# Token inputs transposed two blocks ahead of their splits, and raw token weights loaded later

## The chip, the cores and the metric

The kernel runs on one core of a Trainium2 chip. The metric is the device time of one execution in microseconds (us). Five engines work side by side, each through its own list of instructions in order: TensorE (PE in the rows; PEld is its weight load), VectorE (DVE), ScalarE (ACT), GpSimd (POOL) and SyncE (SP), which here issues every DMA. An instruction may wait on a semaphore of another engine or of a DMA, and then everything behind it on its own engine waits too.

## What is computed

Three layers follow each other on 4 batches of 576 tokens, 512 wide:

```python
scores = scale * np.matmul(q, k.transpose(0, 1, 3, 2))          # 8 heads of 64
bias = np.maximum(x @ w1 + b1, 0.0) @ w2                        # 576 x 576 per head, from positions
attn = softmax(scores + bias);  x = np.matmul(attn, v)          # to 4 x 576 x 512

xt = x.transpose(0, 2, 1)                                       # token mixing
h = np.maximum(xt @ w_tok1, 0.0) @ w_tok2                       # 576 -> 256 -> 576
u = x + h.transpose(0, 2, 1)
x = u + np.maximum(u @ w_ch1, 0.0) @ w_ch2                      # channels, 512 -> 1536 -> 512

# then a gated layer: w_in, tanh form, normalisation, w_sg over tokens, w_out, residual
```

The weights of the second layer reach the kernel as 64-bit floats, seen as pairs of 32-bit words.

## The kernel before, in words

**Attention.** The work is cut into 80 units: a batch, a pair of heads and a block of 128 query tokens (the fifth block has 64). The first 20 units (U0) are batch 0, during which the bias is also made. A unit goes through `scores` (L444: TensorE products `ss`, then a DVE pass at L465 that adds the bias and finds the extreme), `softmax` (L474, ACT), `divisor` and `divided` (L483 to L495, POOL and DVE), `turn_z` and `turn` (L511, L530: TensorE transposes into `z`, `x`, `y`, copied out to `zA`, `xA`, `yA` by ACT or DVE), and `values` (L547: TensorE products `o`, moved to X by `place`, L437). Units -3 to 15 run one at a time in `single` (L704), units 16 (PA) to 77 two at a time in `double` (L752), and units 78 and 79 by the lines after the loops (L808 on). The order of the work is the order of these lines; no planner moves it.

**Bias.** 36 groups of 16 rows are made on TensorE (`bps`), copied by ACT into a staging tile `bst` (L379) and sent by DMA into `bias_m` (L385). Each `single` up to n = 11 makes two. The DVE pass of `scores` waits for the rows of its block.

**Loads.** `loads(n)` (L680) issues all other transfers of unit n on the SP list, behind that unit's bias transfers: K and Q blocks (`kr`, `qr`, four DMAs each, L264), V, and at n = WL (9) the first two raw tiles of the token weights (L95).

**Token weights.** `Jobs` (L64) turns a raw 64-bit tile (`wraw`, two buffers) into a high and a low part. There are seven token jobs: two and a short one for w_tok1, four for w_tok2. A job is worked off in four pieces (`piece`, L158): the ACT square L132 with the DVE operation L133, then L139, L144, L149; the ACT copy L105 and the DVE subtraction L113 of the finished job come with the pieces of the next. A piece is called in `single` for n = 14 and 15 (L742) and at the end of 20 of the 31 `double` calls (L797). What is left is done after the first half of the token product (L831).

**Token inputs.** For batch 0 the tokens are five blocks (0 to 3 and NM, the short one). `x_part` (L616) makes four TensorE transposes of a block into a PSUM tile `px` and then splits it into a high part (ACT, L61) and a low part (DVE, L62), both into space of `bias_m` that is no longer read. A `px` tile holds two blocks and comes from `s_tile` (L353), which deals out two PSUM buffers in turn; `ss`, `px` and the product tiles `ph` share them. `early_x` (L639) takes one or two blocks:

```python
def early_x(ts):
    px = s_tile("px")
    for i, t in enumerate(ts):
        x_part(0, t, x0, px[:, i])
```

It is called with block 0 before the values of units 76 and 77 (L810), and with blocks 1 and 2, then 3 and NM, after the transposes of units 78 and 79 (L824). Then come the values of 78 and 79, the two halves of the first token product (`tok1`, L625, 14 matmuls each into `ph`), the rest of the weight jobs, and `tok1_out` (L633, ACT and DVE), on which the second token product (`pu`, L908) waits.

Of the kernel before, what the change touches and what calls it, by code (L numbers as in the profile page):

```python
# [19 lines left out]
def kernel(ctx, tc, ins, consts, out, dbg=None, nb=4, stop=None):  # L20
# [4 lines left out]
    B, H, N, HD = q.shape  # L25
    P = 128
    NP = H // 2
    NM = N // P
# [30 lines left out]
    def split(src, hi, lo, eng=None):  # L59

        S.copy(out=hi, in_=src)  # L61
        (eng or V).tensor_tensor(out=lo, in0=src, in1=hi.bitcast(F32), op=ALU.subtract)  # L62

    class Jobs:  # L64
# [8 lines left out]
        def add(self, key, nm, rows, cols, fold, dst, times=1):  # L73

            t = ins[nm][rows, cols]
            if fold > 1:
                t = t.rearrange("(a p) c w -> p a c w" if wide[nm] else "(a p) c -> p a c", a=fold)
            else:  # L80
                t = t.rearrange("p (a c) w -> p a c w" if wide[nm] else "p (a c) -> p a c", a=1)
            self.queue.append((key, t, wide[nm], dst, times))
# [110 lines left out]
    U, U0 = len(units), NP * NS  # L193
# [51 lines left out]
    for i in range(NP // 2):  # L245
        t = pp.tile([P, 2 * N + TL], F32, tag="p", name="kraw0")
# [108 lines left out]
    def s_tile(name):  # L355
        flip[0] ^= 1
        return ps_s.tile([P, 2, 512], F32, tag=f"s{1 - flip[0]}", name=name)

    t = pp.tile([P, 2 * N + TL], F32, tag="p", name="early")
# [84 lines left out]
    def scores(n, between):  # L444
        b, p, it = units[n]
        qt, kt = queries.pop(n), keys[b, p]
        na = 2 if it < NM else 1
        if na == 2:
            flip[0] = 0
        ss = [s_tile("ss") for a in range(na)]  # L450

        for hf in range(2):
            js = slice(hf * HN, (hf + 1) * HN)
            for m in range(na):
                for a in range(2):
                    r, o = halves[a], halves[m if na == 2 else a]
                    T.matmul(  # L457
                        ss[a % na][o, hf, 0:HN], lhsT=qt[r, m * HD:(m + 1) * HD], rhs=kt[r, js], start=True, stop=True
                    )
        bias = [bias_m[:, it, 2 * p + a] for a in range(2)] if na == 2 else [bias_t[:, p]]  # L460
        pr = pp.tile([P, 2 * N + TL], F32, tag="p", name="pr")
        mn = sm_p.tile([P, 2], F32, tag="mn", name="mn")
        sm = sm_p.tile([P, 2], F32, tag="sm", name="sm")
        for a in range(na):
            V.tensor_tensor_reduce(  # L465
                out=pr[:, a * NB:a * NB + N].rearrange("p (f n) -> p f n", f=2), in0=ss[a][:, :, 0:HN],
                in1=bias[a].rearrange("p (f n) -> p f n", f=2),
                scale=scale, scalar=BIG, op0=ALU.add, op1=ALU.min, accum_out=mn[:, a:a + 1],
            )
            if a == 0:  # L470
                between()
        return pr, mn, sm, na
# [24 lines left out]
    def normalise(*s):  # L497
        divisor(*s)
        divided(*s)
# [17 lines left out]
    def z_out(n, z, r):  # L517
        zs = rooms[0][2][:, n % 2]
        S.copy(out=zs[r], in_=z[r])
        if units[n][2] < NM:  # L520
            for i in range(2):
                G.tensor_copy(out=zwA[halves[i], n % 2], in_=zs[halves[1 - i], HD:P])
# [20 lines left out]
    def y_out(ys, y):  # L543
        if y is not None:
            V.tensor_copy(out=ys, in_=y)  # L545
# [32 lines left out]
    def hide(gi):  # L578
        if gi < GALL:
            hs[gi] = hidden(groups[gi])  # L580
# [32 lines left out]
    bias_place(groups[GUP - 1], bps)  # L613
    gnext = GUP

    def x_part(b, t, xs, px):  # L616

        w = min(P, N - t * P)
        c0 = b * N + t * P
        for d in range(ND):  # L620
            T.transpose(px[0:w, d * P:(d + 1) * P], X[:, d, c0:c0 + w], ident)

        split(px[0:w], xs[0][0:w, t], xs[1][:, t] if w == P else xs[0][w:2 * w, t])

    def tok1(xs, m, ph):  # L625
        ms = slice(m * P, (m + 1) * P)
        for t in range(NM):
            for n, (i, j) in enumerate(TERMS):
                T.matmul(ph, lhsT=t1[i][:, t, ms], rhs=xs[j][:, t], start=t == 0 and n == 0, stop=False)  # L629
        T.matmul(ph, lhsT=t1[0][:, NM, ms], rhs=xs[0][:, NM], start=False, stop=False)  # L630
        T.matmul(ph, lhsT=t1[1][:, NM, ms], rhs=xs[0][:, NM], start=False, stop=True)
# [7 lines left out]
    def early_x(ts):  # L639
        px = s_tile("px")  # L640
        for i, t in enumerate(ts):
            x_part(0, t, x0, px[:, i])

    tokw = t1 = t2 = None
    wjobs = Jobs(stg, 2)
# [14 lines left out]
            )  # L660
    KL, QL, KT, QT = 11, 10, 7, 6
    st = {}
    PA, PB, WL = U0 - 4, U - 2, 9

    def k_blocks(n):
        for m in range(NP, len(pairs)):
# [37 lines left out]
    def single(n):  # L704
        nonlocal gnext
        gs = []
        if n >= -3 and gnext < GALL:
            gs = list(range(gnext, min(gnext + 2, GALL)))
            gnext += 2
        st[n + 3] = scores(n + 3, (lambda: normalise(*st[n + 2])) if n + 2 >= 0 else (lambda: None))  # L710
        if len(gs) > 0:
            hide(gs[0] + 2)
        if n >= 0:
            z = ps_t.tile([P, 1, P], F32, tag="z", name="z")
            z_out(n, z[:, 0], turn_z(n, st[n][0], z[:, 0]))
            x_out, ys, y = turn(n, st[n][0])
            x_out()
        qs = s_tile("bps") if 0 <= n + 5 < U0 else None
        zq = None if qs is None else qs[:, 0, HN:HN + P]
        q_turn(n + 5, zq)  # L720
        bp = [bias_product(gi, hs.pop(gi), qs if gi == gs[0] else None) for gi in gs]
        if qs is not None and not gs:
            q_out(n + 5, zq)
        softmax(*st[n + 3], which=(0,))
        if n >= 0:
            y_out(ys, y)
        for gi, ps in zip(gs, bp):
            bias_place(groups[gi], ps)
            if gi == gs[0]:
                q_out(n + 5, zq)  # L730

        late = n > 0
        if late and not gs:
            add = values(n - 1)
        softmax(*st[n + 3], which=(1,))
        if late and gs:
            add = values(n - 1)
        if len(gs) > 1:
            hide(gs[1] + 2)
        k_blocks(n)  # L740
        q_blocks(n)
        if n > PA - 3:  # L742
            wjobs.piece()
        if late:
            add()
        st.pop(n - 1, None)
        loads(n)

    def two_values(n):
        return [values(n, "xz"), values(n + 1, "oy")]  # L750
# [56 lines left out]

    flat = bias_m.rearrange("p i h n -> p (i h n)").bitcast(F32R)  # L808
    x0 = [flat[:, i * NS * DM:(i + 1) * NS * DM].rearrange("p (t n) -> p t n", t=NS) for i in range(2)]
    early_x([0])  # L810
    adds = two_values(PB - 2)
    normalise(*st[U - 1])
    for add in adds:
        add()
    z = ps_t.tile([P, 1, P], F32, tag="z", name="z")
    z_out(PB, z[:, 0], turn_z(PB, st[PB][0], z[:, 0]))
    x_out, ys, y = turn(PB, st[PB][0])
# [3 lines left out]
    z_out(U - 1, z[:, 0], turn_z(U - 1, st[U - 1][0], z[:, 0]))  # L821
    x_out, _, _ = turn(U - 1, st[U - 1][0], "o")
    x_out()
    early_x([1, 2])  # L824
    early_x([3, NM])
    for add in two_values(PB):
        add()
    wjobs.need(("t1", NM // 2))
# [67 lines left out]
    if True:  # L896
# [22 lines left out]
        for b in range(nb):  # L919
# [17 lines left out]
            xs = new_x() if b + 1 < nb else None  # L937
# [471 lines left out]
```

## Time and profile before

| what | us |
|---|---|
| median of 3 runs | 885.73 (885.43 to 885.96) |
| the profiled execution, whole | 884.51 |
| its span, first to last instruction | 882.6 |
| PE busy | 867.3 (98% of the span) |
| DVE, ACT, POOL busy | 623.3, 420.8, 231.7 |
| mean granted TensorE clock | 0.997 of full |

All times in rows are microseconds from the start of the span. A row of the timeline reads: start, duration, engine, source line, operation, output<-input, partitions x elements, how many of them were merged, and in brackets how long the engine stood idle just before and what ended that. PE's matmuls are pipelined: the duration of one reaches into the next. The granted clock is a share of full speed (2.4 GHz).

### The profile page before, as it was taken

Reading aid. Unit: us, or ns where it says so; the run is one execution under the profiler, and the core shown is the slowest. Engines: PE = TensorE matmul, PEld = TensorE weight load, DVE = VectorE, ACT = ScalarE, POOL = GpSimd, SP = SyncE. Lnnn points to the kernel's source line nnn. Section 1 sums busy time; section 2 is a strip of 40 time slices with the busy share of each in tenths; the row PEclk is TensorE's granted clock in tenths of the full one; section 3 lists DMA queues with packets and bytes.
Section 4 is the critical chain, followed back from the end, with each engine's and each line's share of the span. In section 5 each row is a group of like instructions: output and inputs, shape, how many; then the busy total and the mean of one; then the engine's idle time right before and its main releaser. Section 6 shows DMA issues by size and latency. Waiting matters only on the chain.

```text
span 882.6 us, 22049 instructions
## 1 busy us (share of the span) xinstructions
PE 867.3 (98%) x8962; PEld 767.3 (87%) x8962; DVE 623.3 (71%) x1429; ACT 420.8 (48%) x955; POOL 231.7 (26%) x440
## 2 busy tenths in 40 slices
PE   8999999999999899999999999999999999999998
PEld 4466688788888789999999999999998989889996
DVE  7899788888787579989836453522218989887756
ACT  7999778888888634343313122212115522322310
POOL 1345467666766400000000000000002422322230
PEclk9999999999999999999999999999999999999999
DMA  8965643344332032234301100000041001010002
GB/s 189 192 138 130 138 80 60 69 76 85 59 65 53 3 96 69 76 117 127 107 34 49 48 25 25 25 1 1 1 81 48 25 1 48 1 61 1 1 13 95
DMA packets 120149, 55.38 MB, mean 63 GB/s; under 512 B 101872, under 2 KB 108656, under 8 KB 120048
## 3 DMA queue, kind: packets, MB, share of 16 engines
q1 hardware_dynamic: 119888, 53.85, 25.5%
q8 instruction: 70, 1.15, 0.6%
q14 instruction: 31, 0.25, 0.1%
q10 hardware_dynamic: 160, 0.13, 0.1%
HBM read 38.62 MB, written 4.72 MB: 49 GB/s over the span
## 4 chain that ended last, share of the span: by engine, by line
PE 86%; DVE 8%; ACT 3%; issue 1%; DMA 1%; POOL 0%; ACTq 0%; DVEq 0%; POOLq 0%
PE a L1040 17%; PE pg L876 17%; PE ss L457 9%; PE o L559 5%; PE pu L1207 5%; PE ps L1229 5%; PE po L1260 4%; PE pv L1154 4%; PE x L535 4%; PE y L540 3%; PE bps L366 3%; PE o L560 2%; PE z L514 2%; PE pu L908 1%; PE ph L629 1%
## 5 line engine op out<-in xcount | busy, mean ns | idle before, releaser
L1040 PE MATMUL a<-g,c 128*128 128x384 f32 x864 | 161.5, 334 | 0.0
L1040 PEld LDWEIGHTS a<-g,c 128*128 128x128 f32 x864 | 151.1, 188 | 0.0
L492 POOL TENSOR_SCALAR pr<-pr,sm 128x576 f32<-128x576 f32 (+2 forms) x208 | 131.2, 648 | 49.6 <-DVE sm L485 42.1
L883 DVE SCALAR_TENSOR_TENSOR g<-pg,g 128x384 fp32r<-128x384 f32 x72 | 40.1, 556 | 146.7 <-ACT g L882 146.7
L876 PE MATMUL pg<-u,c 128*128 128x384 f32 x720 | 134.5, 334 | 0.0
L876 PEld LDWEIGHTS pg<-u,c 128*128 128x128 f32 x720 | 125.7, 188 | 0.1
L882 ACT ACTIVATE g<-pg 128x384 fp32r<-128x384 f32 x72 | 35.3, 491 | 182.6 <-PE pg L876 175.1
L478 ACT ACTIVATE pr<-pr,mn 128x576 f32<-128x576 f32 x144 | 112.4, 780 | 8.0 <-DVE mn L465 6.4
L465 DVE CUSTOM_DVE_ANT_0 pr<-ss,bias_m 128x576 f32<-128x576 f32 x128 | 94.2, 750 | 21.5 <-PE ss L457 17.0
L62 POOL TENSOR_TENSOR y<-X,y 128x576 fp32r<-128x576 f32 x4 | 6.1, 1555 | 367.1 <-ACT y L61 367.1
L559 PE MATMUL o<-xA,vm 64*64 64x128 f32 (+1 forms) x1280 | 80.4, 264 | 0.0
L559 PEld LDWEIGHTS o<-xA,vm 64*64 64x64 f32 x1280 | 69.8, 135 | 10.9 <-issue 5.5
L457 PE MATMUL ss<-kt,X 64*64 64x288 f32 x864 | 71.8, 410 | 0.0
L995 DVE STREAM_TRANSPOSE res<-X 32x256 f32<-32x256 f32 (+1 forms) x176 | 68.2, 387 | 2.9
L560 PE MATMUL o<-yA,vm 64*64 64x128 f32 x1024 | 69.9, 275 | 0.0
L132 ACT ACTIVATE sq<-wraw 128x512 f32<-128x512 f32 (+2 forms) x43 | 27.9, 648 | 66.4 <-DVE w L149 54.7
L560 PEld LDWEIGHTS o<-yA,vm 64*64 64x64 f32 x1024 | 57.7, 134 | 0.7 <-DVE yA L545 0.2
L1229 PE MATMUL ps<-wsT,vn 128*128 128x288 f32 x384 | 56.4, 295 | 0.0
L347 DVE TENSOR_SCALAR X<-ttab,wsm 128x576 f32<-128x576 f32 x108 | 55.3, 572 | 0.1
L1229 PEld LDWEIGHTS ps<-wsT,vn 128*128 128x128 f32 x384 | 52.8, 188 | 0.3 <-POOL vn L62 0.3
L1207 PE MATMUL pu<-y,wi 128*128 128x288 f32 x384 | 51.8, 295 | 1.0 <-ACT uT L1211 1.0
L1207 PEld LDWEIGHTS pu<-y,wi 128*128 128x128 f32 x384 | 51.3, 188 | 1.6 <-ACT uT L1211 1.3
(168 smaller groups left out, 1652.1 us busy)
## 6 DMA issues: line engine op xcount, KB each, us to landing
wraw<-in_moe_w_ch_dram SPq DMA_DIRECT2D x24, 512.0 KB, 3.6
bias_m<-bst SPq DMA_DIRECT2D x32, 288.0 KB, 4.0
vm<-in_v_dram SPq DMA_DIRECT2D x32, 128.0 KB, 2.7
wraw<-in_moe_w_in_dram SPq DMA_DIRECT2D x8, 512.0 KB, 3.6
out_dram<-res SPq DMA_DIRECT2D x16, 256.0 KB, 2.0
kr<-in_k_dram SPq DMA_DIRECT2D x48, 72.0 KB, 2.4
qr<-in_q_dram SPq DMA_DIRECT2D x48, 72.0 KB, 2.5
wraw<-in_moe_w_out_dram SPq DMA_DIRECT2D x4, 512.0 KB, 3.4
```

Of the source, the lines that this page charges most:

```text
L347: V.tensor_scalar(out=hd, in0=tt, scalar1=b1i, scalar2=None, op0=ALU.min)
L457: T.matmul(ss[a % na][o, hf, 0:HN], lhsT=qt[r, m * HD:(m + 1) * HD], rhs=kt[r, js], start=True, stop=True)
L465: V.tensor_tensor_reduce(out=pr[:, a * NB:a * NB + N].rearrange("p (f n) -> p f n", f=2), in0=ss[a][:, :, 0:HN], in1=bias[a].rearrange("p ...
L478: S.activation(out=pr[:, a * NB:a * NB + N], in_=pr[:, a * NB:a * NB + N], func=AF.Exp, scale=-1.0, bias=mn[:, a:a + 1], accum_out=sm[:, a ...
L492: G.tensor_scalar(out=pr[:, dc:dc + hi - lo], in0=pr[:, lo:hi], scalar1=sm[:, a:a + 1], scalar2=1.0, op0=ALU.mult, op1=ALU.mult,)
L559: T.matmul(o[0:HD, 0:w], lhsT=vm[r, t, 0], rhs=xs[r, t, 0:w], start=st_, stop=en)
L560: T.matmul(o[HD:P, 0:w], lhsT=vm[r, t, 1], rhs=rh[r], start=st_, stop=en)
L876: T.matmul(pg, lhsT=c1[f][i][:, d], rhs=u[j][:, d], start=d == 0 and n == 0, stop=d == ND - 1 and n == 2)
L995: V.transpose(out=o, in_=src(c)[32 * a:32 * a + 32])
L1040: T.matmul(acc[d], lhsT=c2[f][i][:, d * P:(d + 1) * P], rhs=g[j], start=f == f0 and n == 0, stop=f == f1 and n == 2,)
L1207: T.matmul(pu[:, hf, 0:HN], lhsT=wi[i][:, d, f * P:(f + 1) * P], rhs=y[j][:, d, js], start=d == 0 and m == 0, stop=d == ND - 1 and m == 2,)
L1229: T.matmul(ps[:, hf, 0:HN], lhsT=vn[i][:, t, ds_], rhs=wsT[j][:, t, js], start=t == 0 and m == 0, stop=False,)
```

## The change

Five things are edited. `x_part` is cut into `x_turn` (transposes) and `x_split`; `early_x` transposes all its blocks first and returns the splits to be called later. Block 1 is now transposed with block 0, before the values of units 76 and 77, and split after them; blocks 2 and 3 share a tile, and NM has one for itself. `WL` becomes U0 - 6 = 14. The two calls of `piece` in `single` are gone.

```diff
+    def x_turn(b, t, px):
+        c0 = b * N + t * P
         w = min(P, N - t * P)
-        c0 = b * N + t * P
         for d in range(ND):
             T.transpose(px[0:w, d * P:(d + 1) * P], X[:, d, c0:c0 + w], ident)
 
+    def x_split(t, xs, px):
+        w = min(P, N - t * P)
         split(px[0:w], xs[0][0:w, t], xs[1][:, t] if w == P else xs[0][w:2 * w, t])
...
     def early_x(ts):
         px = s_tile("px")
         for i, t in enumerate(ts):
-            x_part(0, t, x0, px[:, i])
+            x_turn(0, t, px[:, i])
+        return [lambda i=i, t=t: x_split(t, x0, px[:, i]) for i, t in enumerate(ts)]
...
-    PA, PB, WL = U0 - 4, U - 2, 9
+    PA, PB, WL = U0 - 4, U - 2, U0 - 6
...
         q_blocks(n)
-        if n > PA - 3:
-            wjobs.piece()
         if late:
...
-    early_x([0])
+    xsplits = early_x([0, 1])
+    xsplits[0]()
     adds = two_values(PB - 2)
     normalise(*st[U - 1])
     for add in adds:
         add()
+    xsplits[1]()
...
-    early_x([1, 2])
-    early_x([3, NM])
+    xsplits = early_x([2, 3]) + early_x([NM])
+    for f in xsplits:
+        f()
     for add in two_values(PB):
```

Three places show how the instructions move. On SP, near the end of the bias (`wraw` is a raw weight tile, `bst` the bias staging tile):

```order
 L385 DMA bias_m<-bst 16x8x576 x2
 L264 DMA kr<-in_k_dram 32x18x32 x4
-L95 DMA wraw<-in_moe_w_tok_dram 128x2x512 x2
 L385 DMA bias_m<-bst 16x8x576 x2
 L264 DMA qr<-in_q_dram 32x18x32 x4
 L385 DMA bias_m<-bst 16x8x576 x2
+L264 DMA kr<-in_k_dram 32x18x32 x4
+L95 DMA wraw<-in_moe_w_tok_dram 128x2x512 x2
+L264 DMA qr<-in_q_dram 32x18x32 x4
```

The two raw tiles went from ahead of the last two pairs of bias transfers to behind them and behind the next K block, ahead of the Q block that follows it.

On PE, after the transposes of the last unit (x is its attention turned, px the token inputs, o the values; the brackets name the engine whose semaphore an instruction waits for):

```order
 L535 MATMUL x<-ident,pr 128x128 [waits DVE_49]
 L535 MATMUL x<-ident,pr 128x128 x3
-L621 MATMUL px<-ident,X 128x128 x4
-L621 MATMUL px<-ident,X 128x128 [waits DVE_49]
-L621 MATMUL px<-ident,X 128x128 x7
-L621 MATMUL px<-ident,X 64x128 [waits DVE_49]
-L621 MATMUL px<-ident,X 64x128 x3
+L620 MATMUL px<-ident,X 128x128 x8
+L620 MATMUL px<-ident,X 64x128 [waits DVE_49]
+L620 MATMUL px<-ident,X 64x128 x3
```

Sixteen transposes with two waits for DVE became twelve with one; the other four stand earlier, behind those of block 0.

On ACT, the same stretch, before and then in the changed kernel (L61 makes the high part of a block, L441 moves values, L519 and L541 copy a unit's turned attention):

```order
L61 CAST bias_m<-px 128x512 [waits PE_49]
L441 COPY X<-o 128x128 [waits PE_49] x2
L519 COPY zA<-z 128x128 [waits PE_49]
L541 COPY xA<-x 128x512 [waits PE_49,Activation_49]
L519 COPY zA<-z 64x128 [waits PE_49]
L541 COPY xA<-x 128x512 [waits DVE_49,PE_49]
L61 CAST bias_m<-px 128x512 [waits PE_49]
L61 CAST bias_m<-px 128x512 [waits DVE_49,PE_49]
L61 CAST bias_m<-px 128x512 [waits PE_49]
L61 CAST bias_m<-px 64x512 [waits DVE_49,PE_49]
```

```order
L61 CAST bias_m<-px 128x512 [waits PE_49]
L441 COPY X<-o 128x128 [waits PE_49] x2
L61 CAST bias_m<-px 128x512 [waits DVE_49]
L519 COPY zA<-z 128x128 [waits PE_49]
L541 COPY xA<-x 128x512 [waits PE_49,Activation_49]
L519 COPY zA<-z 64x128 [waits PE_49]
L541 COPY xA<-x 128x512 [waits PE_49]
L61 CAST bias_m<-px 128x512 [waits PE_49]
L61 CAST bias_m<-px 128x512 [waits DVE_49]
L61 CAST bias_m<-px 64x512 [waits PE_49]
```

The cast of block 1 moved ahead of the copies of units 78 and 79, and the casts of blocks 1 and 3, the second of their tiles, wait for DVE.

## Rows read from the trace of the kernel before

**Rows 1.** TensorE's waits from 98 us on: total, times, longest, us.

```profile
PE px L621 <- DVE bias_m L62: 3.0, 2, 1.6
PE bps L416 <- DVE mn L465: 1.8, 1, 1.8
...
PE pu L908 <- DVE h L635: 1.0, 2, 0.5
```

**Rows 2.** Timeline of SP from 80 us: DMA issues.

```profile
87.29 1.18 SPq L95 DMA_DIRECT2D wraw<-in_moe_w_tok_dram  x2
88.98 1.43 SPq L385 DMA_DIRECT2D bias_m<-bst  x2
90.51 6.28 SPq L264 DMA_DIRECT2D qr<-in_q_dram  x4
96.89 1.73 SPq L385 DMA_DIRECT2D bias_m<-bst  x2
104.97 1.94 SPq L264 DMA_DIRECT2D kr<-in_k_dram  x4
```

**Rows 3.** DMA issues from 88.9, 96.8 and 121.4 us: count, KB, us to landing.

```profile
bias_m<-bst SPq DMA_DIRECT2D x2, 288.0 KB, 8.4
...
bias_m<-bst SPq DMA_DIRECT2D x2, 288.0 KB, 3.9
...
kr<-in_k_dram SPq DMA_DIRECT2D x4, 72.0 KB, 2.4
```

**Rows 4.** Timeline of ACT, PE and DVE, 94 to 104 us.

```profile
94.58 0.83 ACT L379 ACTIVATE bst<-bps,evb,over_c 128x576 f32<-128x576 f32 x1
...
98.87 1.15 PE L457 MATMUL ss<-kt,q 64*64 64x288 f32 x16
...
102.15 0.76 DVE L465 CUSTOM_DVE_ANT_0 pr<-ss,bias_m 128x576 f32<-128x576 f32 x1 [2.36 <-DMA bias_m<-bst]
...
102.97 0.33 PE L416 MATMUL bps<-ident,qm 128*128 128x128 f32 x1 [1.81 <-DVE mn L465]
```

**Rows 5.** Timeline of DVE, 104 to 122 us: pieces of the weight jobs.

```profile
108.56 0.43 DVE L133 TENSOR_SCALAR w<-wraw 128x512 int32<-128x512 int32 x1
...
116.35 0.68 DVE L144 SCALAR_TENSOR_TENSOR w<-wraw,w 128x512 int32<-128x512 int32 x1
```

**Rows 6.** Timelines of PE, DVE and ACT, 294 to 309 us.

```profile
295.12 0.19 PEld L559 LDWEIGHTS o<-xA,vm 64*64 64x64 f32 x2 [0.17 <-ACT pr L478]
...
299.13 0.60 PE L621 MATMUL px<-ident,X 128*128 128x128 f32 x4
...
300.44 0.69 DVE L62 TENSOR_TENSOR bias_m<-px,bias_m 128x512 fp32r<-128x512 f32 x1 [0.96 <-ACT bias_m L61]
...
301.18 1.09 PE L621 MATMUL px<-ident,X 128*128 128x128 f32 x8 [1.45 <-DVE bias_m L62]
...
301.88 1.07 ACT L61 CAST bias_m<-px 128x512 fp32r<-128x512 f32 x2 [1.47 <-PE px L621]
...
302.50 1.29 DVE L62 TENSOR_TENSOR bias_m<-px,bias_m 128x512 fp32r<-128x512 f32 x2 [1.37 <-ACT bias_m L61]
...
303.84 1.06 PE L621 MATMUL px<-ident,X 128*64 128x128 f32 x4 [1.56 <-DVE bias_m L62]
...
307.63 1.66 PE L629 MATMUL ph<-bias_m,t 128*128 128x512 f32 x6
```

**Rows 7.** Windows: us, PE, PEld, DVE, ACT, POOL busy, granted clock, DMA share, GB/s.

```profile
101.00:103.00 2.00, 0.19 (x3) 0.04 (x1) 0.85 (x4) 0.40 (x1) 0.00 (x0) 1.00 0.04 6
...
304.00:305.00 1.00, 1.00 (x8) 0.54 (x11) 0.00 (x0) 0.07 (x1) 0.00 (x0) 0.50 0.12 25
```

**Rows 8.** Timeline of DVE, 304 to 330 us: weight pieces, then both h parts.

```profile
308.06 0.45 DVE L144 SCALAR_TENSOR_TENSOR w<-wraw,w 128x288 int32<-128x288 int32 x1
...
312.17 0.69 DVE L635 SCALAR_TENSOR_TENSOR h<-ph,h 128x512 fp32r<-128x512 f32 x1
315.10 0.69 DVE L635 SCALAR_TENSOR_TENSOR h<-ph,h 128x512 fp32r<-128x512 f32 x1 [2.24 <-ACT h L634]
```

More of the change, by code (lines that the diff above doesn't have):

```diff
@@ L614, with x_part @@
     gnext = GUP
-    def x_part(b, t, xs, px):
+    def x_turn(b, t, px):
+        c0 = b * N + t * P
         w = min(P, N - t * P)
-        c0 = b * N + t * P
         for d in range(ND):
             T.transpose(px[0:w, d * P:(d + 1) * P], X[:, d, c0:c0 + w], ident)
+    def x_split(t, xs, px):
+        w = min(P, N - t * P)
         split(px[0:w], xs[0][0:w, t], xs[1][:, t] if w == P else xs[0][w:2 * w, t])
+    def x_part(b, t, xs, px):
+        x_turn(b, t, px)
+        x_split(t, xs, px)
     def tok1(xs, m, ph):
```

## The prediction

> **What bounds the kernel.** I read the list of TensorE's waits first, because PE is 98% busy: only a gap on PE, or slow PE work, can be won. From 98 us on the list holds little [rows 1]: two waits of the token transposes `px` for the DVE part of a split (3.0 us), one wait of `bps` for the DVE pass L465 (1.8 us), two of `pu` for h (1.0 us). The change touches the places of the first two. The rest of the reading follows these two gaps back: the one near 101 us through DVE to a DMA and to the SP list [rows 2 to 4], the ones near 300 us through DVE and ACT [rows 6]. The windows show what TensorE's clock did around each [rows 7], the last rows whether other work then stands in the way [rows 5, 8].
>
> **A: the raw weights leave the path of the last bias rows.** Before, SP issues the two raw tiles at 87.29, then a bias pair at 88.98 that takes 8.4 us to land, while the pair at 96.89 takes 3.9 [rows 2, 3]. Behind it four Q issues take 6.28 us, where four like ones of K take 1.94 later [rows 2]: SP is held up while the transfers ahead drain. So the last bias pair is issued at 96.89 to 98.62, although ACT had made its second half by 94.58 + 0.83 = 95.41 [rows 4]. L465 reads it at 102.15, after 2.36 us of idle, and PE's `bps` follows after 1.81 idle [rows 4]. In the changed order nothing raw stands ahead: Q issues from 90.5 to about 92.5, the second bias half at about 95.45, landing 3.9 later, at 99.4. L465 also needs its score products, done at 98.87 + 1.15 = 100.02 [rows 4], and then starts at about 100.1, which is 2.05 earlier. PE's own earlier work lets it gain its 1.81 idle and little more: I take 1.9, bounds 0 (the first rival) and 2.05.
>
> **B: two pieces leave units 14 and 15.** These units form a chain through DVE, POOL and PE. One of the DVE operations taken out, 0.43 long at 108.56, stood ahead of a pass L465 [rows 5]; the other, like it or longer, stood beside POOL's copies. Most of each fits into waits on other engines. I take 0.3, bounds 0 and 0.86 (two of 0.43). The pieces do not vanish: every later piece moves two calls on, among `double` calls in which PE has no listed wait [rows 1], so I cost that at nothing. If that cover were gone it would cost some tenths per call. The last two pieces fall into the tail (D).
>
> **C: the split chain at the end of attention.** Before, PE issues block 1's four transposes at 299.13. Eight take 1.09 and four 0.60 in the rows, so the spacing is about 0.11 and four occupy 0.44 [rows 6]. PE stands from 299.57 to 301.18 for the DVE split of block 1 (300.44 + 0.69), makes eight, stands from 302.06 to 303.84 for that of block 3, and begins the token product at 307.63 [rows 6]. From 303.84 to 307.63 it worked 3.8 us, nearly all at a granted clock of 0.50 [rows 7]: about 3.3 us of it, so at full speed this work is about 2.1 us, and 1.7 of it without the NM transposes.
>
> In the changed kernel the first gap is gone, since blocks 2, 3 and NM are written before any of their splits; block 1's split is early, so NM need not wait for it. Twelve transposes from about 299.2 (0.07 lost, because block 1's cast stands ahead of unit 78's copies on ACT) end at 300.5, and the values of 78 and 79 end at about 300.5 + 1.7 = 302.2. The split chain is now beside them: both blocks of the tile are written by 299.2 + 0.88 + 0.27 = 300.3; the cast starts, the subtraction follows 0.62 later (301.88 to 302.50) and takes 0.69 [rows 6], so block 2 is done at 301.6. Block 3's cast waits for DVE, as its order row says; counting DVE's increments in the program, it is the subtraction of block 2. So block 3 is done 0.05 + 0.62 + 0.69 later, at 303.0. The first matmul of the token product writes the PSUM buffer in which these blocks lay, and waits until then: 0.8 us of idle remain. Start 303.0 instead of 307.63: 4.6 won. Bounds: 3.0 if the clock still falls (second rival), 5.4 if nothing waits.
>
> Block 1's four transposes now stand ahead of the values of 76 and 77. PE idles 0.17 there [rows 6], and these values wait for ACT's copies in any case. No row shows how much more is covered: bounds 0 and 0.44, I take 0.1 lost.
>
> **D: the tail of weight work.** Before, DVE works on weights from 308.06 until h at 312.17, 4.1 us [rows 8]. Two pieces more bring three more DVE operations of at most 0.46: 5.5 us. They start when the split of NM and the last additions are done, at about 303.9 in C's scale, and end at 309.4. DVE is next needed by the second h part, at 315.10 - 4.6 = 310.5 [rows 8]. Hidden, with 1.1 us to spare. If it were not, each us beyond would move `pu` by one. The raw tiles needed there are loaded some pieces before. The w_ch loads start when a raw buffer is free; that shifts by about as much as their use.
>
> **Sum.** 1.9 + 0.3 + 4.6 - 0.1 = 6.7 us. Behind the token product the list of PE's waits has nothing that is tied to the old time [rows 1], so the gain should reach the end. The profiled execution, 884.51, becomes 877.8; its median stands 1.2 higher, so the median goes from 885.73 to **879.0**. With the bounds the forecast reaches from 877.2 (2.05 + 0.86 + 5.4 + 0 = 8.3, rounded out) to 881.5.
>
> **Rivals.**
>
> *The bias stall stays.* Then the lateness is not due to the raw tiles but to K and Q, whose pieces are 32 floats wide. Against it: four K transfers of that shape land in 2.4 us with no raw tile ahead [rows 3]. For it: 288 KB of them still stand ahead of each bias pair. A is 0, time 880.9. The Trainium skill, "DMA: Bandwidth & Descriptors", section Specifications, says that 512 B is the least for full rate and that below it the engine reads, modifies and writes; by that rule K and Q stay slow and A could be lost. Chance 8%.
>
> *The clock still falls.* PE keeps a gap of 0.8 us. Two gaps of 1.6 and 1.8 us within five brought 0.50 at 304 [rows 6, 7]; one gap of 1.8 us at 101 left 1.00 [rows 7], so one of 0.8 should. If it fell for as long as before, 3.3 us at half clock cost 1.6: time 880.6. The Trainium skill, "TensorE: Matmul & The Clock Gate", Part 1, says that the throttled state is the default and activity lifts it; by that rule any idle stretch counts against the change. Chance 10%.
>
> *Slower: the first raw tile comes late.* Its first piece now stands in the first `double`, on ACT and DVE, whose lists hold the softmax behind it. It takes the place of L144 at 116.35 [rows 5], about 114.1 in the new time. The raw issue follows four K issues that before began at 104.97 [rows 2], now 103.1, so at 105.0. It holds nothing up unless it lands more than 9.1 us later; the longest landing here is 8.4 [rows 3]. Beyond that each us costs one. To end 1.8 us slower it must eat 6.7 + 1.8, a landing of 17.6 us: time 887.5. Chance 3%.
>
> **How the numbers follow.** Forecast 76%, stall stays 8%, clock falls 10%, slower 3%, and 3% that a wait not listed here eats the gain. About 0.2% (1.8 us) is what a measurement can tell from no change. The first three are faster: 0.94; same 0.03, slower 0.03. The first two rivals lie at 880.9 and 880.6, inside 877.2 to 881.5, which is the range.
>
> **What would show it.** Right: no wait of L465 for a bias DMA; L133 first at about 114; no wait of `px` for DVE over 0.1 us, but one of about 0.8 us at the first `ph` matmul; the granted clock at 1.00 through that stretch; the token product beginning 6.7 us earlier, near 300.9; `pu` waiting for h as before. Wrong: a bias landing over 4.6 us after the last issue (A); a clock of 0.50 after the transposes (C); `pu` waiting longer, with DVE in weight pieces just before (D); an ACT or DVE wait for a raw tile near 114 (the slower rival).

## The result and the profile after

The changed kernel takes **877.56 us** (median, 876.78 to 877.84, 4 runs) where the kernel before takes 885.58 beside it (883.9 to 885.96, 4 runs): a ratio of **0.9912, interval 0.9895 to 0.9929**. The profiled execution went from 884.51 to 876.78, its span from 882.6 to 874.8.

TensorE's waits of the changed kernel from 96 us on (total, times, longest, us):

```profile
PE pu L1215 <- ACT uT L1219: 1.0, 1, 1.0
PE pu L916 <- DVE h L641: 1.0, 2, 0.5
PE ph L635 <- DVE bias_m L62: 0.7, 1, 0.7
```

Against [rows 1], the two waits of `px` (3.0 us) and the wait of `bps` (1.8) are gone, those of `pu` for h stand as they stood, and one new wait is there: 0.7 us of the first token product for a split. (The wait at L1215 lies in the gated layer, which is not edited.)

The timeline of SP in the changed kernel, 86 to 112 us (start, duration, issues):

```profile
88.00 1.73 SPq L385 DMA_DIRECT2D bias_m<-bst  x2
89.82 2.43 SPq L264 DMA_DIRECT2D qr<-in_q_dram  x4
93.49 1.51 SPq L385 DMA_DIRECT2D bias_m<-bst  x2
102.25 2.23 SPq L264 DMA_DIRECT2D kr<-in_k_dram  x4
104.52 1.02 SPq L95 DMA_DIRECT2D wraw<-in_moe_w_tok_dram  x2
106.04 3.20 SPq L264 DMA_DIRECT2D qr<-in_q_dram  x4
```

This answers to [rows 2]. The four Q issues near 90 us take 2.43 us instead of 6.28, and the last bias pair is issued from 93.49 instead of 96.89. The hold-up has not vanished: the four Q issues behind the raw tiles now take 3.20 us, and the next rows show that their landing takes 5.4. Nobody waits for them there.

DMA issues of the changed kernel from 93 and from 102 us (count, KB, median us to landing):

```profile
bias_m<-bst SPq DMA_DIRECT2D x2, 288.0 KB, 4.7
...
wraw<-in_moe_w_tok_dram SPq DMA_DIRECT2D x2, 512.0 KB, 4.9
kr<-in_k_dram SPq DMA_DIRECT2D x4, 72.0 KB, 2.6
qr<-in_q_dram SPq DMA_DIRECT2D x4, 72.0 KB, 5.4
```

DVE and PE of the changed kernel where the stall was, and the first piece of a weight job (start, duration, in brackets the idle time ahead):

```profile
99.42 0.76 DVE L465 CUSTOM_DVE_ANT_0 pr<-ss,bias_m 128x576 f32<-128x576 f32 x1 [0.61 <-PE z L514]
...
100.25 0.33 PE L416 MATMUL bps<-ident,qm 128*128 128x128 f32 x1
...
113.01 0.42 DVE L133 TENSOR_SCALAR w<-wraw 128x512 int32<-128x512 int32 x1
```

Before, the first of these rows was released by a DMA after 2.36 us [rows 4]; now it is released by PE, and `bps` has no idle time ahead. The first piece finds its raw tile there.

PE, DVE and ACT of the changed kernel at the end of attention, 291 to 309 us:

```profile
291.14 1.04 PE L620 MATMUL px<-ident,X 128*128 128x128 f32 x8
...
296.00 1.47 PE L620 MATMUL px<-ident,X 128*128 128x128 f32 x12
...
297.69 0.69 DVE L62 TENSOR_TENSOR bias_m<-px,bias_m 128x512 fp32r<-128x512 f32 x1 [1.23 <-ACT bias_m L61]
...
298.41 1.06 ACT L61 CAST bias_m<-px 128x512 fp32r<-128x512 f32 x2 [0.76 <-DVE bias_m L62]
...
299.03 1.41 DVE L62 TENSOR_TENSOR bias_m<-px,bias_m 128x512 fp32r<-128x512 f32 x2 [0.65 <-ACT bias_m L61]
...
299.87 3.04 PE L635 MATMUL ph<-bias_m,t 128*128 128x512 f32 x12 [0.68 <-DVE bias_m L62]
...
300.81 0.45 DVE L113 TENSOR_TENSOR t<-w,t 128x288 fp32r<-128x288 f32 x1
...
305.69 0.46 DVE L113 TENSOR_TENSOR t<-w,t 128x288 fp32r<-128x288 f32 x1 [0.50 <-ACT t L105]
306.19 0.69 DVE L641 SCALAR_TENSOR_TENSOR h<-ph,h 128x512 fp32r<-128x512 f32 x1
307.30 0.69 DVE L641 SCALAR_TENSOR_TENSOR h<-ph,h 128x512 fp32r<-128x512 f32 x1 [0.42 <-ACT h L640]
```

Twelve transposes run in one go where [rows 6] had eight between two gaps. ACT's second cast waits 0.76 us for DVE's first subtraction, and the token product waits 0.68 for the second subtraction of the same tile. The weight work fills DVE from 300.81 to 306.15; the second h follows 0.42 us of idle, so that work is hidden.

Windows of the changed kernel (us, PE, PEld, DVE, ACT, POOL busy, granted clock, DMA share, GB/s):

```profile
300.00:302.00 2.00, 2.00 (x9) 1.64 (x10) 1.91 (x6) 0.11 (x1) 0.00 (x0) 1.00 0.00 0
302.00:304.00 2.00, 2.00 (x10) 1.59 (x10) 1.72 (x5) 0.78 (x2) 0.00 (x0) 1.00 0.14 18
```

The granted clock stays at 1.00 (2.4 GHz), where the kernel before had 0.50 (1.2 GHz) at 304 to 305 [rows 7].

**Where the 7.8 us of the span lie.** The 144 passes L465 on DVE stand in the same order in both kernels, so they can be used as milestones. I count them from 0; number 28 is the pass at which the bias stall was, number 143 the last. Each cell is the difference of two starts on the DVE timeline, in us:

| from, to | before | changed | gained |
|---|---|---|---|
| start of the span to pass 0 | 19.56 | 18.54 | 1.02 |
| pass 0 to 28 (bias stall, A) | 82.59 | 80.88 | 1.71 |
| 28 to 30 | 3.32 | 3.33 | 0.0 |
| 30 to 34 (single units 14 and 15, B) | 8.60 | 7.98 | 0.62 |
| 34 to 143 | 178.61 | 178.50 | 0.11 |
| 143 to the second h (C) | 22.42 | 18.07 | 4.35 |
| second h to the end of the span | 567.5 | 567.5 | 0.0 |

No edited line runs in the first 19 us. Three profiled executions of the unchanged kernel reach pass 0 at 19.56, 18.70 and 18.79, three of the changed kernel and a near copy at 18.54, 18.92 and 19.24; the 1.02 belongs to these two executions and not to the change. The edits account for 6.8 us of this pair of profiles.

### The profile page after: what moved, and what is told of

The parts are those of the page before. It is cut to its first block, busy times and chain, and to the rows that moved or that the text cites. A ratio compares the mean times of both kernels' runs of the same rounds, so it can differ in the third digit from the quotient of the medians.

```text
span 874.8 us, 22050 instructions
## 1 busy us (share of the span) xinstructions
PE 864.3 (99%) x8962; PEld 766.0 (88%) x8962; DVE 623.2 (71%) x1429; ACT 420.6 (48%) x955; POOL 230.2 (26%) x440
## 3 DMA queue, kind: packets, MB, share of 16 engines
q8 instruction: 70, 1.15, 0.6%
## 4 chain that ended last, share of the span: by engine, by line
PE 86%; DVE 9%; ACT 2%; issue 1%; DMA 1%; SPq 0%; DVEq 0%; ACTq 0%
PE a L1048 17%; PE pg L884 17%; PE ss L457 9%; PE o L559 5%; PE pu L1215 5%; PE ps L1237 5%; PE po L1268 4%; PE pv L1162 4%; PE x L535 4%; PE y L540 3%; PE bps L366 3%; PE o L560 2%; PE z L514 2%; PE pu L916 1%; PE ph L635 1%
## 5 line engine op out<-in xcount | busy, mean ns | idle before, releaser
L465 DVE CUSTOM_DVE_ANT_0 pr<-ss,bias_m 128x576 f32<-128x576 f32 x128 | 94.3, 751 | 19.9 <-PE ss L457 17.2
L1215 PE MATMUL pu<-y,wi 128*128 128x288 f32 x384 | 51.8, 295 | 1.0 <-ACT uT L1219 1.0
L1215 PEld LDWEIGHTS pu<-y,wi 128*128 128x128 f32 x384 | 51.4, 188 | 1.6 <-ACT uT L1219 1.3
```

The source lines that it names most:

```text
L465: V.tensor_tensor_reduce(out=pr[:, a * NB:a * NB + N].rearrange("p (f n) -> p f n", f=2), in0=ss[a][:, :, 0:HN], in1=bias[a].rearrange("p ...
L1215: T.matmul(pu[:, hf, 0:HN], lhsT=wi[i][:, d, f * P:(f + 1) * P], rhs=y[j][:, d, js], start=d == 0 and m == 0, stop=d == ND - 1 and m == 2,)
```

## The experiments

The ratios are to the kernel before on the same chip; the eleven runs below came in three groups, one chip each. The changed kernel was timed again in the first group alone, so the two kernels made from it in the second (other tiles, still later load) are compared with it across chips. The kernel before had medians of 884.37, 885.1 and 884.4 us there, and its 58 executions spread from 881.57 to 889.41. My theory: the three edits act by A (raw tiles hold up SP and with it the last bias pair), B (two pieces out of a chain) and C (gaps of PE and the clock behind them), and these add up. The rivals were those of the forecast; what was open was the size of each, and what makes the kernel before spread.

### The changed kernel again

No edit; the first group is compared with it.

> The changed kernel as it is, timed again beside the kernel before on one chip. Theory: the three places of the change (bias stall 1.75, two pieces 0.6, split chain 4.4 by the two profiles) are all there is, and the 1.0 us by which the changed kernel is ahead already at 20 us, before any edited line, belongs to the execution: 6.7 us faster, between 6.0 and 7.3. Rival: the early 1.0 comes with the change every time: 7.8 to 8.2 us faster.

Measured: 877.24 us (877.06 to 878.17, 6 runs), ratio 0.9929 [0.9911, 0.9947]. That is 7.1 under the kernel before, inside the 6.0 to 7.3 of the theory and under the 7.8 to 8.2 of the rival. The interval, 4.7 to 7.9 us, just takes in the rival's lower end; what speaks against it are the starts of pass 0 given above. Pass 143 to the second h takes 18.08, pass 30 to 34 takes 7.99, as in the first profile.

### The later load undone

```diff
-    PA, PB, WL = U0 - 4, U - 2, U0 - 6
+    PA, PB, WL = U0 - 4, U - 2, 9
```

> The changed kernel with the raw token weights loaded at n = 9 again, ahead of the last two bias pairs; nothing else undone. Theory: the bias stall comes back, TensorE idles 1.8 us at bps near 101 us, and the kernel is 1.8 us slower than the changed one (4.9 faster than before). Rival, the lateness was due to the K and Q blocks: no stall here, same time as the changed kernel.

Measured: 879.25 us (878.36 to 880.52, 8 runs), 2.0 over the changed kernel beside it. PE's waits and two rows of SP, of the changed kernel with the early load:

```profile
PE bps L416 <- DVE mn L465: 2.0, 1, 2.0
PE ph L635 <- DVE bias_m L62: 0.7, 1, 0.7
```

```profile
89.78 6.36 SPq L264 DMA_DIRECT2D qr<-in_q_dram  x4
96.24 1.90 SPq L385 DMA_DIRECT2D bias_m<-bst  x2
```

The number 6.28 of [rows 2] is back as 6.36, and the `bps` wait with it. The stall is the raw tiles' doing. Both vary from execution to execution: in the seven profiles with both raw tiles ahead the four Q issues take 6.05 to 7.01 us and PE waits 1.5 to 2.4, the longest wait with the longest issues.

### Half of the raw bytes early

The kernel before, but one raw tile at unit 9 and the other at unit 13:

```diff
-        def load(self):
-            while len(self.loaded) < self.ahead and self.next + len(self.loaded) < len(self.queue):
+        def load(self, most=2):
+            while len(self.loaded) < min(most, self.ahead) and self.next + len(self.loaded) < len(self.queue):
...
+            wjobs.load(1)
+        if n == PA - 3:
```

> The kernel before, with one raw token-weight tile (512 KB) issued at unit 9 and the second one at unit 13, behind the last bias pair; pieces and splits as before. Theory (the bytes of the raw tiles ahead hold up the Q issues on SP and the bias pair behind them): about half of the hold-up stays, so the four Q issues near 90 us take 3 to 5 us instead of 6.28, the last bias pair is issued 1.5 to 3 us earlier, TensorE's wait of bps for the pass L465 falls from 1.8 to under 0.9 us or vanishes, and L465 number 28 moves 1 to 2 us earlier against the start. The median is then 1 to 2 us under that of the kernel before. Rival (the narrow K and Q blocks are the cause, whatever raw bytes stand there): the Q issues still take over 6 us, the wait stays at 1.8 us, the time is that of the kernel before within 0.5 us.

Measured: 881.68 us (880.59 to 883.87, 11 runs), ratio 0.9962 [0.9944, 0.998]. SP, and PE's wait near 101 us, of the half load:

```profile
86.99 0.68 SPq L95 DMA_DIRECT2D wraw<-in_moe_w_tok_dram  x1
88.70 1.43 SPq L385 DMA_DIRECT2D bias_m<-bst  x2
90.22 3.49 SPq L264 DMA_DIRECT2D qr<-in_q_dram  x4
94.18 1.51 SPq L385 DMA_DIRECT2D bias_m<-bst  x2
```

```profile
PE bps L416 <- DVE mn L465: 0.5, 1, 0.5
```

With two raw tiles ahead the four Q issues take 6.28 us and PE waits 1.8; with one, 3.49 and 0.5; with none, 2.43 and nothing. So the hold-up of SP goes with the bytes in the queue ahead. The rival of the narrow K and Q blocks fell: they are the same in all three. Pass 0 to 28 takes 81.31 us, 1.3 less than in the first profile of the kernel before, as expected; the median gained 3.4 (1.8 to 5.0 by the interval) where 1 to 2 was expected. One execution in eleven has a mean clock of 0.996 or less here, 29 of 58 in the kernel before; whether the smaller stall or chance did that is not shown.

### Only the new splits

The changed kernel with the load at unit 9 and the two pieces put back:

```diff
-    PA, PB, WL = U0 - 4, U - 2, U0 - 6
+    PA, PB, WL = U0 - 4, U - 2, 9
...
         q_blocks(n)
+        if n > PA - 3:
+            wjobs.piece()
```

> The kernel before with the new split order alone: load at n = 9 and both pieces in the single units. Theory: 4.4 us faster than before (4.0 to 4.7), the clock at 1.00 through the stretch, one wait of about 0.7 us at the first ph matmul. Rival, the gain needs the earlier edits too (fewer pieces near the end): under 3.5 us.

Measured: 879.31 us (878.88 to 880.97, 6 runs), ratio 0.9953 [0.9935, 0.9972]: 5.1 under the kernel before by the medians, over the 4.0 to 4.7 expected, with an interval of 2.5 to 5.8 us that takes them in. Pass 143 to the second h takes 18.07 us, the same as with everything: C depends on the splits alone. The `bps` wait is 1.8 again and the `px` waits are gone.

### Only the pieces

The kernel before without the two calls:

```diff
-        if n > PA - 3:
-            wjobs.piece()
```

> The kernel before with the two pieces of units 14 and 15 taken out, so that they fall to the tail; nothing else. Theory: 0.3 to 0.7 us faster than before, all of it between 107 and 113 us. Rival, the two pieces come back in the tail, where they stand between the split chain and h: within 0.2 us of before or slower.

Measured: 882.23 us (880.96 to 886.55, 12 runs), ratio 0.9986 [0.997, 1.0003]: the median can't tell it from no change, because the executions spread too far. The milestones can: pass 30 to 34 falls from 8.60 to 7.99, as in the changed kernel, and pass 143 to the second h stays at 22.45. B is 0.6 us.

### Only the later load and the pieces

The kernel before with `WL = U0 - 6` and without the two calls; transposes and splits as before:

```diff
-    PA, PB, WL = U0 - 4, U - 2, 9
+    PA, PB, WL = U0 - 4, U - 2, U0 - 6
...
-        if n > PA - 3:
-            wjobs.piece()
```

> The kernel before with the later load (WL = U0 - 6) and without the two pieces in the single units; the transposes and splits of the token inputs as before. Theory (A, B and C add up, and C carries the spread): the wait of bps for L465 is gone, L465 number 28 to number 34 as in the changed kernel, the two px waits stay at 3.0 us; the median is 1.5 to 3 us under that of the kernel before, at full clock about 879.4 (882.0 less 2.4), and the executions still spread over 4 us or more, with mean clocks down to 0.995. Rival (the bias stall has a part in the clock falls, since the half-load kernel with both px gaps and a stall of 0.5 us had one execution in eleven at 0.996 or less): the executions spread over 3 us or less, with hardly any mean clock under 0.997, and the median is 3 to 5 us under that of the kernel before.

Measured: 881.42 us (879.64 to 883.46, 12 runs), ratio 0.9962 [0.9947, 0.9977], 3.0 under the kernel before. The `bps` wait is gone, the `px` waits are 3.0. Its executions spread over 3.8 us with mean clocks from 0.996 to 1.000, none lower: between the two expectations. So the gaps at the end of attention are enough for clock falls: in its profile, at 0.996, pass 143 to the second h takes 23.55 us instead of 22.42. Mean clocks of 0.994 and 0.995 were seen only in the two kernels that have both the full bias stall and these gaps (the kernel before, and the one with only the pieces out). The looks below show why.

### Two looks at the kernel before

No edit; the aim was to see where executions of unlike mean clock differ.

> The kernel before, unchanged, one more profiled execution. Theory (the 7 us over which its executions spread are clock lost behind the two px gaps, for a stretch of another length each time): if this execution has a mean granted clock of 0.996 or less, the windows show it below 1.00 in one stretch that begins at 302 to 304 us and lasts 8 us or more, the way from the last pass L465 to the second h is 23 us or more (22.4 at 0.997, 20.9 where the clock stays up), and all other distances are those of the first profile within 0.3 us. If its mean clock is 0.999 or 1.000, that way is 20.9 us. Rival (the clock is lost somewhere else): the way is 22.4 us or less at a mean clock of 0.996 or under, and another stretch, near the bias stall at 101 us or behind 320 us, shows the low clock.

> The kernel before, unchanged, a further profiled execution, to see a second length of the clock fall. The same two readings as for the look ahead of it: way from the last pass L465 to the second h of 20.9 us plus about half of the time that the windows show at 0.50 (theory), or a low clock in another place (rival).

They fell on the two ends: 886.39 us at a mean clock of 0.994, and 881.96 at 0.999. Windows of the execution at 0.994:

```profile
103.00:105.00 2.00, 2.00 (x46) 1.77 (x44) 1.15 (x2) 0.80 (x3) 1.46 (x5) 0.50 0.04 8
...
304.00:306.00 2.00, 1.42 (x12) 0.96 (x16) 0.53 (x1) 0.32 (x1) 0.00 (x0) 0.50 0.05 12
306.00:308.00 2.00, 2.00 (x60) 2.00 (x56) 0.68 (x1) 0.42 (x2) 0.00 (x0) 0.50 0.00 0
```

The same windows at 0.999:

```profile
103.00:105.00 2.00, 2.00 (x42) 1.38 (x35) 1.71 (x4) 1.62 (x6) 1.40 (x5) 1.00 0.05 12
...
304.00:306.00 2.00, 2.00 (x64) 1.80 (x57) 1.62 (x5) 0.49 (x3) 0.00 (x0) 1.00 0.04 12
306.00:308.00 2.00, 2.00 (x11) 1.59 (x10) 1.82 (x5) 0.79 (x2) 0.00 (x0) 1.00 0.43 98
```

The waits of PE are nearly the same in both (`px` 3.0 and 3.0, `bps` 1.9 and 1.5). But in the first the clock fell to 0.50 behind each of the two stalls, in the second behind neither, and in the profile of [rows 7] behind the later one only. What each fall costs is read from the milestones, us:

| kernel before, mean clock | 28 to 30 | 143 to second h | span |
|---|---|---|---|
| 0.999 | 3.32 | 20.89 | 880.1 |
| 0.997 (the first profile) | 3.32 | 22.42 | 882.6 |
| 0.994 | 4.95 | 23.58 | 884.5 |

The two falls together cost 1.63 + 2.69 = 4.3 us, and the spans differ by 4.4. My theory had named one place; there are two. (It had also expected 8 us or more at 0.50 in the one place; the way of 23 us or more came true, with 0.50 from 304 to 310.)

### The gaps filled with unused work

The kernel before with 14 and 15 more transposes into a tile that nobody reads, behind those of blocks 1 and 3:

```diff
+            if i == 0 and fill:
+                spare_z = ps_t.tile([P, P], F32, tag="z", name="fz")
+                for j in range(fill):
+                    T.transpose(spare_z, X[:, j % ND, 0:P], ident)
...
-    early_x([1, 2])
-    early_x([3, NM])
+    early_x([1, 2], 14)
+    early_x([3, NM], 15)
```

> The kernel before, with TensorE given unused work in the two gaps at the end of attention: 14 more transposes behind those of block 1 and 15 behind those of block 3, into a spare tile that nobody reads. Nothing is removed; the splits, the loads and the pieces are as before. Theory (the two gaps let TensorE's clock fall, and how long it then stays down differs from execution to execution): the granted clock stays at 1.00 through 300 to 308 us, the token product begins about 1.6 us earlier than before against the last pass L465, the median falls by 1.5 us or more, and the executions of this kernel lie within 2 us of each other where those of the kernel before spread over 5. Rival (the spread comes from the bias stall, from the start or from the chip, and the clock fall is worth less than the forecast said): the clock still falls or the executions spread over 4 us or more as before, and the median is within 1 us of the kernel before. The two waits of px for the DVE split stay in the list in both cases, shorter by what the added transposes fill.

Measured: 882.9 us (881.82 to 884.95, 12 runs), ratio 0.9975 [0.9959, 0.9992]: 2.2 less by the medians, for doing more. PE at the end of attention, with the fill in the `fz` rows:

```profile
300.46 0.60 PE L621 MATMUL px<-ident,X 128*128 128x128 f32 x4
300.90 1.69 PE L646 MATMUL fz<-ident,X 128*128 128x128 f32 x14
302.51 1.10 PE L621 MATMUL px<-ident,X 128*128 128x128 f32 x8
303.44 1.80 PE L646 MATMUL fz<-ident,X 128*128 128x128 f32 x15
```

```profile
304.00:306.00 2.00, 2.00 (x25) 1.64 (x27) 1.11 (x2) 0.45 (x2) 0.00 (x0) 1.00 0.00 0
```

The granted clock stays at 1.00 at 304 to 306, the two `px` waits are gone from PE's list (they were expected to be shorter), and pass 143 to the second h takes 20.91 us, as in the execution at 0.999. So the way through the gaps at full clock is 20.9, and C's 4.35 is 2.84 of gaps (20.91 - 18.07) and 1.51 of clock in the first profile. Its twelve executions lie at mean clocks of 0.997 and above, where 29 of the 58 of the kernel before lie at 0.996 or below. They still spread over 3.1 us, more than the 2 expected; the bias stall is still in this kernel (2.4 us in its profile).

### The last blocks dealt out otherwise

The changed kernel with block 3 alone in its tile, and blocks 2 and NM together:

```diff
-    xsplits = early_x([2, 3]) + early_x([NM])
+    xsplits = early_x([3]) + early_x([2, NM])
```

> The changed kernel, with the last token blocks dealt out to the two PSUM buffers in another way: block 3 alone in one tile and blocks 2 and NM together in the other, so that the tile that the first token product writes is free after one split instead of two. Theory (the 0.7 us that TensorE still waits at the first ph matmul is the second split of a shared tile): that wait falls from 0.7 to under 0.2 us, the first h comes about 0.6 us earlier against the last pass L465 (16.4 instead of 16.96), and the median is 0.3 to 0.7 us under the 877.2 to 877.6 of the changed kernel. Rival (the wait only moves to the second ph tile, to the split of the last block or to the weight pieces): the first h may come earlier, but second and third h stand where they stood, and the time is that of the changed kernel within 0.2 us.

Measured: 876.86 us (876.53 to 879.51, 6 runs), ratio 0.9902 [0.988, 0.9923]. PE's waits, and the row of the first token product:

```profile
PE pu L916 <- DVE h L641: 1.0, 2, 0.5
...
PE bps L416 <- DVE mn L465: 0.2, 1, 0.2
```

```profile
300.23 3.06 PE L635 MATMUL ph<-bias_m,t 128*128 128x512 f32 x12
```

The wait of `ph` is gone. The second h begins 17.35 us after pass 143 instead of 18.07 (it is merged with the first into one row that starts at 307.01 and lasts 1.36; half of that is 0.68), and the third h 29.95 instead of 30.69. So 0.7 us are won that are not lost again behind. The two h operations now follow the weight work on DVE without idle time, so that work is what they wait for next. By medians it stands 0.4 to 0.7 under the changed kernel, with intervals that overlap: the trace shows this step, the medians alone don't.

### The load later still

The changed kernel with `WL = U0 - 4`, behind the Q block of the first pair:

```diff
-    PA, PB, WL = U0 - 4, U - 2, U0 - 6
+    PA, PB, WL = U0 - 4, U - 2, U0 - 4
```

> The changed kernel with the raw token weights loaded one unit pair later (WL = U0 - 4 = 16), behind the K block of the first pair call. Theory (the forecast's slower rival has its margin: nothing is held up while the first raw tile lands before ACT and DVE come to the first piece near 113 us, and beyond that each us costs one): the raw issues move from 104.5 to 107 to 110 us, the landing of about 5 us then ends at 112 to 115, so the first piece waits 0 to 2 us for its tile and the time is 0 to 1.5 us over that of the changed kernel (877 to 879). Rival (the placing of the load does not matter beyond the bias, because the softmax behind the piece has slack): a wait for the raw tile shows on ACT or DVE, but TensorE gets no new wait and the time is that of the changed kernel within 0.3 us.

Measured: 877.92 us (877.19 to 879.7, 6 runs). The issue on SP and the first piece on DVE:

```profile
109.04 2.38 SPq L95 DMA_DIRECT2D wraw<-in_moe_w_tok_dram  x2
...
114.03 0.43 DVE L133 TENSOR_SCALAR w<-wraw 128x512 int32<-128x512 int32 x1
```

The raw issue moves by 4.5 us, the landing still takes 5.0 (median of the two tiles), and the first piece stands where it stood: 2.28 us behind pass 34 in both (113.01 - 110.73 and 114.03 - 111.75), with no idle time for the raw tile. The expected wait did not come: the first tile landed at 113.47, 0.6 us ahead of its piece, and in the changed kernel at 108.83, 4.2 us ahead. So the slower rival of the forecast was 4 us away. The median is 0.4 to 0.7 over those of the changed kernel on other chips; no milestone from pass 28 on differs by more than 0.1.

## Why the prediction was right, and where it was off

**The bound and the reach of the gain.** PE's list of waits was the right place to look: everything gained lies at waits of that list, in clock behind them, or in B, part of which is a wait of the weight loads (PEld) that this list leaves out. Behind the second h both kernels take 567.5 us.

**A** was 1.9 forecast, 1.71 measured (1.43 against the execution at 0.999, whose wait was 1.5): the term was of the right size, within what the stall varies. The mechanism is shown by the early load put back and by the half load. One of my signs for "wrong" came true without harm: the last bias pair took 4.7 us to land, over the 4.6 I had allowed, but it was issued 3.4 us earlier. The rival that the stall stays fell: 72 KB of K or Q in pieces of 32 floats land in 2.4 to 2.6 us when nothing large stands ahead, and the pass at the stall (number 28) is released by PE and no longer by a DMA. The Trainium skill, "DMA: Bandwidth & Descriptors", Specifications, names 512 B as the least transfer for full rate. These pieces are 128 B in every kernel here, so no run shows what their size costs; the half load shows that with the same pieces the bytes ahead decide how long they hold SP up.

**B** is the term that was mis-sized: "0.3, bounds 0 and 0.86" where 0.62 was measured in the changed kernel and 0.61 with the pieces alone taken out. I had assumed that "most of each fits into waits on other engines", and I had priced the second DVE operation like the first, at 0.43. The rows show it longer, and a POOL copy slowed beside it on which PE's weight loads wait. The kernel before:

```profile
111.12 1.16 DVE L139 SCALAR_TENSOR_TENSOR w<-wraw,w 128x512 int32<-128x512 int32 x1
...
111.81 0.86 POOL L522 COPY zwA<-zA 64x64 f32<-64x64 f32 x2
...
112.43 0.42 PEld L566 LDWEIGHTS o<-zwA,vt 64*64 64x64 f32 x3 [0.30 <-POOL zwA L522]
```

The changed kernel, without the piece:

```profile
108.81 0.52 POOL L522 COPY zwA<-zA 64x64 f32<-64x64 f32 x2
```

Pass 30 to 32, with the first operation, fell by 0.27 (3.63 to 3.36). Pass 32 to 34, with the second, fell by 0.35 (4.97 to 4.62), and POOL's copies by 0.34. All six profiles with both pieces show this operation at 1.15 to 1.17 us; later in the kernel before, away from these copies, the same operation on 128x512 takes 0.68. Why the two slow each other is not shown.

**C** was 4.6 less 0.1, against 4.35. The token product was forecast at 300.9; it began at 299.87 in an execution that started 1.02 earlier, so at 300.89. The remaining idle time was forecast at 0.8 and is 0.68, by the path given: the cast of block 3 waits for the subtraction of block 2. (The two durations from which I took a spacing of 0.11 give 0.12; twelve transposes in 1.47 us bear out the 0.11.) The clock's part was forecast at 1.6 and is 1.5 in that profile.

**D**: 5.5 us forecast, 5.3 measured, and hidden; the margin to the second h is 0.42 us instead of 1.1, and with the other tiles it is used up.

**The sum** was 6.7, and the edits account for 6.8 of the profiled pair. The upper end of my range, 881.5, does not follow from the terms' lower bounds, which leave 2.6 us of gain (0 + 0 + 3.0 - 0.44) and a time of 883.2; it was set by the rivals. The median gained more than 6.7, namely 8.0, and the step that failed there is the one from the profile to the median: I took the profile's clock fall as the kernel's. It is one draw. Another part of the 8.0 is the draw too: the four executions of the kernel before in that comparison have a median of 885.58, the 58 others 884.74. At a mean clock of 1.000 eight executions of the kernel before lie at 881.58 to 882.53 (median 882.05), eight of the changed kernel and of its copy with the still later load at 877.16 to 878.34 (median 877.39): 4.7 us from gaps and pieces, where the milestones against the execution at 0.999 give 4.9. Over all executions the medians are 884.74 (58) and 877.39 (16), 7.35 apart, so some 2.7 us lie in executions with a lower clock, which the changed kernel hardly has.

**The clock rival** was argued with a wrong premise: "one gap of 1.8 us at 101 left 1.00". It did in that execution; at 0.994 a `bps` wait of 1.9 was followed by 0.50, and so was the one of 1.8 in the kernel with only the new splits (0.63 at 103 to 105, 0.52 at 105 to 107). For the 0.68 us of the changed kernel its executions speak: 15 of 16 at mean clocks of 0.999 and 1.000, and three profiles with no fall behind that wait. The one at 0.998 (879.70 us) was not profiled, so that this wait never brings a fall is not shown.

## What to carry to other kernels

A short gap on TensorE can cost its length and a stretch at half clock behind it, and whether the second happens is a matter of the execution: before costing a clock stretch, list the mean granted clock of every run and compare runs at equal clock. When an engine's transfers are late, look at what stands ahead in the same issue list, also at issues that take long themselves, and move the bulk to where the next consumers are far off. Milestones that both kernels share (here the passes L465) split a difference into its terms where medians can't. Price an instruction that is taken out by its own row at its own place, not by a like one, and look at what the other engines do beside it.

## What the runs showed of the hardware

- **Chance clock falls.** How the executions lie, by what gaps of PE a kernel has (waits from its profile):

| kernel | waits of PE, us | executions | mean clock | us |
|---|---|---|---|---|
| before | `bps` 1.8, `px` 3.0 | 58 | 0.994 to 1.000 | 881.57 to 889.41 |
| only the pieces out | `bps` 1.7, `px` 3.0 | 12 | 0.995 to 1.000 | 880.96 to 886.55 |
| half load | `bps` 0.5, `px` 3.0 | 11 | 0.996 to 1.000 | 880.59 to 883.87 |
| later load, pieces out | `px` 3.0 | 12 | 0.996 to 1.000 | 879.64 to 883.46 |
| gaps filled | `bps` 2.4 | 12 | 0.997 to 1.000 | 881.82 to 884.95 |
| early load, new splits | `bps` 2.0, `ph` 0.7 | 8 | 0.998 to 1.000 | 878.36 to 880.52 |
| only the new splits | `bps` 1.8, `ph` 0.7 | 6 | 0.998 to 1.000 | 878.88 to 880.97 |
| changed, with its copies | `ph` 0.7 | 16 | 0.998 to 1.000 | 876.78 to 879.70 |
| other tiles | `bps` 0.2 | 6 | 0.998 to 1.000 | 876.53 to 879.51 |

The Trainium skill, "TensorE: Matmul & The Clock Gate", Part 1, says of warming up at a kernel's start that it is "run-variable". Here the same is seen of falls in the middle: [rows 7] and the two looks show the same gaps followed by 0.50 in some executions and by 1.00 in others. What decides it in one execution is not shown. Nor is what made the single executions at 0.998 of the kernels without these gaps (879.70 and 879.51) longer; neither was profiled.

- **Unused work that pays.** Twenty-nine transposes that nobody reads made the kernel before 2.2 us quicker by the medians (ratio 0.9959 to 0.9992), and in the profiled execution the clock stayed at 1.00 through both gaps.
- **A queue's issues take longer behind bulk.** Four issues of 72 KB took 6.05 to 7.01 (seven profiles), 3.49 and 2.43 us of SP's time behind 1 MB, 512 KB and nothing of raw weights, each time with a bias pair (576 KB) between, and 3.20 behind 1 MB with none between.
- **A DVE operation and a POOL copy side by side.** The DVE operation of the second piece took 1.15 to 1.17 us instead of 0.68, and the longer of the two POOL copies beside it 0.57 instead of 0.23, in all six profiles that have both.
